# Re-ordering VectorE's top-k steps, loading second-MoE weight pieces ahead, and summing two slot tables on TensorE

## The chip, the cores and the metric

The kernel runs on one core of one Trainium2 chip, in one launch. The metric is device time in microseconds (us); smaller is better. The core has five engines with one in-order instruction queue each: TensorE (PE in the profile), VectorE (DVE), ScalarE (ACT), GpSimd (POOL) and SyncE (SP, which only issues DMAs here; POOL issues the indirect ones).

## The reference, cut to what matters

```python
scores = (q @ k.T) / sqrt(64)                # 4 batches, 8 heads, 576 rows
kth    = 32nd largest score of each row
attn   = softmax(where(scores >= kth, scores, -1e9)) @ v
x = attn as [2304 tokens, 512]
h = x @ w_in;  x = (h * clip(h + 3, 0, 6) / 6) @ w_out            # first MoE, d_ff 2048
logits = x @ w_gate;  e = argmax(logits);  g = softmax(logits)[e]   # 8 experts
out[t] = g[t] * (relu(x[t] @ w1[e]) @ w2[e])                     # second MoE, d_ff 1024
```

## The kernel before, in words

**Attention** goes in 144 tiles of 128 query rows (`T`), one per step of the loop at L1044. A step `t` works on several tiles at once, each at another stage: scores of tile t+2 on TensorE (`qk`) and their copy to SBUF on ScalarE (`sevac`); the search for the 32 largest of tile t on VectorE (`top_a`: eight MAX8 over 72 columns each at L626, then three MAX8 with two MATCH_REPLACE between them, L632 and L637); exponentials and a sign count of tile t-1 on ScalarE; then, for tile t-1, the scores not above the 24th largest (`z`). For the first 20 tiles (`ZPE`) z is made by GpSimd (L669) and TensorE (L596) in the PSUM tensor `yps`; for later ones by one VectorE instruction (L662). For tile t-2 `mask` then does three things on VectorE: MAX8 over z (L697, rank name `max8`), a small instruction that picks the 32nd value (L701, `match`), and the masking of the exponentials (L705, `mask`, two SBUF inputs of 576 columns). Transposes (L721) and the product with v (L755) follow on TensorE. In the first 200 us VectorE, ScalarE and GpSimd also convert the first MoE's weights from 64-bit to 32-bit numbers (`conv64`, L295 to L313).

**The order of the work** is made ahead of time by a planner. Every instruction has a rank: `pr0[0] + PRIO[name]`, where `pr0` grows by 400 a step. Among the instructions that its own model takes to be ready, the planner puts the lowest rank next into each engine's queue. At run time each queue is in order: an instruction whose input is late holds all those behind it.

**The first MoE** is cut into 144 steps (`moe_step`, 9 blocks of 256 tokens times 16 slices of d_ff) that run beside attention and alone after it, from about 850 us on: L829 (first matrix), ScalarE and VectorE (L835, L841), GpSimd (L264, L849), L860 (second matrix). Each step's piece of w_out is loaded by SP (L815). `gate` finds each token's expert, and GpSimd writes token numbers into one of two slot tables in DRAM (`td`, filled beforehand with values from 2304 up).

**The second MoE** takes the experts in turn, 384 token slots each. An expert's weights come in 8 pieces of 512 KB (`wpiece`): even numbers from w1, odd ones from w2. A piece is loaded by SP into one of three buffers `raw` (L967, L970), rounded by ScalarE (L977) and its remainder taken by VectorE (L978). Of expert 0, pieces 0, 2, 4, 6, 1 and 3 are asked for in the loop at L1112, while the first MoE ends; the converted pieces 5 and 7 lie in a pool (`tabp`) that opens only when the first MoE has ended. `load_table` (L951) reads the two tables and VectorE takes their minimum (L955). TensorE transposes it and adds the slots of the last block (L1133, L1135, into `tps`); VectorE turns the sum into the gather indices `tabg` (L1136) and the scatter indices `tab` (L1137). Three indirect DMAs of GpSimd gather the tokens of expert 0 (L1148); TensorE transposes them (L1157), ScalarE and VectorE round them (L1159, L1160), and the matrices follow (L1175, L1192).

Of the kernel before, what the change touches and what calls it, by code (L numbers as in the profile page):

```python
# [13 lines left out]
F32 = mybir.dt.float32  # L14
# [5 lines left out]
ALU = mybir.AluOpType  # L20
# [29 lines left out]
PRIO = dict(  # L50
    load=-1940, epi_a=370, top_c=55, exp=-295, need=75, qk=10, pv=-40, sevac=390, xevac=440, trans=210, xt0=75,
    tevac=450, xt1=-1170, l2=260, sign=175, epi_c=1010, wo=1175, prep=105, top8=270, rounds=-815, epi_b=165, l1=310,
    max8=315, match=560, mask=55, conv=295, xt2=-1335, z=365, gate=525, zw=60, zpe=70, yevac=405, convn=935,
)


# [1 line left out]
def attention_two_moe_kernel(  # L58
# [13 lines left out]
    PE, V, A, G, SP = nc.tensor, nc.vector, nc.scalar, nc.gpsimd, nc.sync  # L72

    B, H, S, D = q.shape
    NT, DM = out.shape
    F1 = w_in.shape[1]
    NE, _, F2 = w1.shape
    P = 128
# [13 lines left out]
    NG = NBLK * NF1  # L92
    YW = DM + 4
    NTT = NT // P
    SLOTS = 3
# [36 lines left out]
    def r_(ap):  # L132
        return ap.bitcast(F32)
# [7 lines left out]
    def run(gen):  # L141
        for _ in gen:
            pass

    cpool = ctx.enter_context(tc.tile_pool(name="cpool", bufs=1))
# [8 lines left out]
    def constants():  # L154
        c = {}
        c["ident"] = ident = cpool.tile([P, P], F32, name="ident")
        c["ntiny"] = ntiny = cpool.tile([P, 1], F32, name="ntiny")

        V.memset(ntiny, -1.02 * TINY2)
        c["one"] = one = cpool.tile([P, 1], F32, name="one")  # L160
        V.memset(one, 1.0)
        c["three"] = three = cpool.tile([P, 1], F32, name="three")
        V.memset(three, 3.0)
        c["tri"] = tri = cpool.tile([P, P], BF16, name="tri")

        make_identity(nc, ident)
        jp = cpool.tile([P, P], I32, name="jp")
        G.iota(jp, pattern=[[1, P]], base=0, channel_multiplier=-1)
        V.tensor_scalar(tri, jp, 0.0, None, op0=ALU.is_gt)
        c["ones"] = ones = cpool.tile([P, P], BF16, name="ones")  # L170
        V.memset(ones, 1.0)
        c["iota8"] = iota8 = cpool.tile([P, NE], F32, name="iota8")
        G.iota(iota8, pattern=[[1, NE]], base=0, channel_multiplier=0, allow_small_or_imprecise_dtypes=True)

        c["isum"] = isum = cpool.tile([P, 8, 2], F32, name="isum")
        G.iota(isum, pattern=[[2, 8], [-1, 2]], base=S - 2 * (TOPK - 1), channel_multiplier=0,
               allow_small_or_imprecise_dtypes=True)
        c["tok"] = tok = cpool.tile([P, NTT], F32, name="tok")
        G.iota(tok, pattern=[[P, NTT]], base=0, channel_multiplier=1, allow_small_or_imprecise_dtypes=True)


        c["row"] = row = cpool.tile([P, P], F32, name="row")
        G.iota(row, pattern=[[1, P]], base=0, channel_multiplier=0, allow_small_or_imprecise_dtypes=True)
        c["first"] = first = cpool.tile([P, NE, SLOTS], F32, name="first")
        G.iota(first, pattern=[[NT, NE], [P, SLOTS]], base=0, channel_multiplier=0, allow_small_or_imprecise_dtypes=True)
        c["tokm"] = tokm = cpool.tile([P, NTT], F32, name="tokm")
        G.iota(tokm, pattern=[[P, NTT]], base=-NT, channel_multiplier=1, allow_small_or_imprecise_dtypes=True)
        c["wg"] = wg = cpool.tile([P, NCC, NE], F32, name="wg")
        c["ohsum"] = cpool.tile([P, NE], BF16, name="ohsum")
        c["flag"] = cpool.tile([P, 2], F32, name="flag")  # L190
        c["ctl"] = cpool.tile([1, 2 + NE], I32, name="ctl")
        c["ctlf"] = cpool.tile([1, 2 + 2 * NE], F32, name="ctlf")
        return c
# [4 lines left out]
    def body(cs, exact):  # L198
        X = "x" if exact else ""
        ident, three, tri, ones, iota8 = cs["ident"], cs["three"], cs["tri"], cs["ones"], cs["iota8"]  # L200
# [747 lines left out]
        NSL = NE * SLOTS  # L948
        placed, gdone, trows, tables = [], [0], [], []

        def load_table():  # L951
            trows.extend(wp[0].tile([NSL, P], F32, name=f"trow{i}") for i in range(2))
            for a_, t_ in zip(trows, td):
                SP.dma_start(a_, t_.rearrange("(e s p) o -> e s (p o)", e=NE, p=P)[:, 0:SLOTS, :])
            V.tensor_tensor(trows[0], trows[0], trows[1], op=ALU.min)  # L955


        NPC = 4
        FW = F2 // NPC
        FPP = NF2 // NPC  # L960
        wst = {}

        def wpiece(e, i):
            kind, pc = i % 2, i // 2
            raw = wp[0].tile([P, 4 * FW], F32, tag="raw", bufs=3, name=f"raw{e}_{i}")
            if kind == 0:
                SP.dma_start(raw.rearrange("p (c f) -> p c f", c=NCC),  # L967
                             w1[e, :, pc * FW:(pc + 1) * FW].rearrange("(c p) f -> p c f", p=P))
            else:
                SP.dma_start(raw.rearrange("p (j n) -> p j n", j=FPP),  # L970
                             w2[e, pc * FW:(pc + 1) * FW, :].rearrange("(j p) n -> p j n", p=P))
            late = kind and pc >= NPC // 2
            nb = 3 if kind else 5
            pool = tabp[0] if late else wp[0]
            h = pool.tile([P, 4 * FW], F32R, tag=f"wh{kind}", bufs=nb, name=f"wh{e}_{i}")
            l = pool.tile([P, 4 * FW], F32R, tag=f"wl{kind}", bufs=nb, name=f"wl{e}_{i}")
            A.activation(h, raw, AF.Copy)  # L977
            V.tensor_tensor(l, raw, r_(h), op=ALU.subtract)  # L978
            wst[e, kind, pc] = (h, l)

        pend = []
        gpos = [0]
# [3 lines left out]
        def moe_step():  # L986
            g = gpos[0]
            if g >= NG + 3 or (g < NG and blkready[0] <= g // NF1):
                return
            gpos[0] += 1  # L990
            if 0 <= g - 1 < NG:
                epi_a(g - 1)
            yield
            if g >= 3:
                l2(g - 3)
                bk, f = divmod(g - 3, NF1)
                if f == NF1 - 1:
                    for tt, y in enumerate(yevac(bk)):
                        pend.append([gate(bk, tt, y), 0])
            yield  # L1000
            if 0 <= g - 1 < NF1:
                conv_upto(2 * (g - 1) + 1)
            if 0 <= g - 1 < NG:
                load_wo(g - 1)
            if 0 <= g - 2 < NG:
                epi_c(g - 2)
            yield
            if 0 <= g - 1 < NG:
                epi_b(g - 1)
            yield  # L1010
            if g < NG:
                if g < NF1:
                    conv_upto(2 * g)
                l1(g)
# [5 lines left out]
        wp, tabp = [None], [None]  # L1020

        def gate_step():
            for g_ in list(pend):

                if g_[1] or g_ is pend[0] or pend[0][1] > 2 or gpos[0] >= NG + 3:
                    g_[1] += 1
                    if next(g_[0], "end") == "end":
                        pend.remove(g_)
# [79 lines left out]
        at.close()  # L1108
        m2 = ExitStack()
        wp[0] = m2.enter_context(tc.tile_pool(name="wp" + X, bufs=1, side="right"))  # L1110
        pre = []
        while gpos[0] < NG + 3 or pend:  # L1112
            pr0[0] += STEP
            run(moe_step())
            gate_step()
            tc.cur_priority = pr0[0] + STEP
            if gdone[0] == NTT - TB // P and not trows:
                load_table()
            if gpos[0] > NG - 12 and len(pre) < NPC + NPC // 2:

                pre.append(2 * len(pre) if len(pre) < NPC else 2 * (len(pre) - NPC) + 1)
                wpiece(0, pre[-1])
        m1.close()
        tc.cur_priority = pr0[0] + 2 * STEP

# [3 lines left out]
        tab = tabp[0].tile([P, NSL], I32, name="tab")  # L1129
        tabg = tabp[0].tile([P, NSL], I32, name="tabg")  # L1130
        tps = ps2.tile([P, NSL], F32, tag="tp", bufs=2, name="tps")

        PE.matmul(tps, trows[0], ident[0:NSL, 0:NSL], start=True, stop=False)  # L1133
        for i, (a_, b_) in enumerate(placed):
            PE.matmul(tps, a_, b_, start=False, stop=(i == len(placed) - 1))  # L1135
        V.tensor_scalar(tabg, tps, float(NT - 1), None, op0=ALU.min)  # L1136
        V.tensor_copy(tab, tps)  # L1137

        xst = {}

# [63 lines left out]
        xgather(0)  # L1204
        for f_ in tables:
            f_()
        for i in range(2 * NPC):
            if i not in pre:
                wpiece(0, i)
# [3 lines left out]
        for s in range(len(seq) + 2):  # L1213
            if s < len(seq):
                e, f = seq[s]
# [33 lines left out]
    def more(cs, e, n):  # L1249
        ident = cs["ident"]  # L1250
        with ExitStack() as st:
# [10 lines left out]
            with tc.For_i(CAP, n, P) as i:  # L1262
# [31 lines left out]
                G.indirect_dma_start(out, bass.IndirectOffsetOnAxis(to, 0), o, None, bounds_check=NT - 1, oob_is_err=False)  # L1294

    cs = constants()
    body(cs, False)
    ctl = control(cs, "")
    big = P * (3 * T + 1) + NE
# [40 lines left out]
```

## Time and profile before

| | us |
|---|---|
| median of 3 runs | 1247.75 |
| lowest and highest of them | 1244.34, 1252.39 |
| the profiled execution: time | 1248.94 |
| the profiled execution: span | 1247.0 |
| TensorE matmul busy (92% of the span) | 1148.2 |
| VectorE busy (75%) | 940.1 |
| ScalarE busy (65%) | 816.1 |
| GpSimd busy (37%) | 461.8 |

The rows quoted below come from the profiled execution. Its span runs from the first to the last instruction; what the time holds beside it, 1.9 us, lies outside. Times in rows count from the start of the span. A row of a timeline gives start, length, engine, line, operation, output<-input, shape and count, and in brackets the idle time before it with what ended it.

### The profile page before, as it was taken

Reading aid. Unit: us, or ns where it says so; the run is one execution under the profiler, and the core shown is the slowest. Engines: PE = TensorE matmul, PEld = TensorE weight load, DVE = VectorE, ACT = ScalarE, POOL = GpSimd, SP = SyncE. Lnnn points to the kernel's source line nnn. Section 1 sums busy time; section 2 is a strip of 40 time slices with the busy share of each in tenths; the row PEclk is TensorE's granted clock in tenths of the full one; section 3 lists DMA queues with packets and bytes.
Section 4 is the critical chain, followed back from the end, with each engine's and each line's share of the span. In section 5 each row is a group of like instructions: output and inputs, shape, how many; then the busy total and the mean of one; then the engine's idle time right before and its main releaser. Section 6 shows DMA issues by size and latency. Waiting matters only on the chain.

```text
span 1247.0 us, 23972 instructions
## 1 busy us (share of the span) xinstructions
PE 1148.2 (92%) x7453; PEld 1033.9 (83%) x7453; DVE 940.1 (75%) x3800; ACT 816.1 (65%) x2089; POOL 461.8 (37%) x670
## 2 busy tenths in 40 slices
PE   6676788999999999999999999999986999999995
PEld 4565677788999899999888899998875999999994
DVE  4999999999999999999897999995423444444420
ACT  4888778687888887787777887784422444444421
POOL 5886555743323534323433323223433112221100
PEclk9678799999999999999999999999996999999998
DMA  3654556555544655645435545444954455555300
GB/s 81 201 163 137 181 187 207 156 140 144 148 125 126 141 155 161 141 124 135 129 99 153 145 121 155 121 121 125 315 170 136 147 171 172 154 163 164 121 19 26
DMA packets 184665, 180.22 MB, mean 145 GB/s; under 512 B 123933, under 2 KB 148813, under 8 KB 184528
## 3 DMA queue, kind: packets, MB, share of 16 engines
q1 hardware_dynamic: 178960, 167.24, 46.4%
q0 software_dynamic: 4416, 11.08, 2.9%
q8 instruction: 61, 1.00, 0.3%
q14 instruction: 76, 0.62, 0.2%
q10 hardware_dynamic: 1152, 0.28, 0.1%
HBM read 160.52 MB, written 19.59 MB: 144 GB/s over the span
## 4 chain that ended last, share of the span: by engine, by line
PE 74%; DVE 14%; ACT 5%; DMA 3%; issue 2%; POOL 2%; SPq 0%; POOLq 0%; ACTq 0%; DVEq 0%
PE l1ps L829 13%; PE yps L860 13%; PE lp L1175 11%; PE ops L1192 11%; PE ptps L755 9%; PE sps L596 5%; PE ptps L721 4%; DVE cd L626 2%; DVE pbuf L705 2%; DVE z L662 2%; DVE z L697 1%; PE ptps L888 1%; DMA raw<-in_moe_w_dram 1%; PE misc L440 1%; PE tp L1157 1%
## 5 line engine op out<-in xcount | busy, mean ns | idle before, releaser
L860 PE MATMUL yps<-wo,gh 128*128 128x512 f32 x576 | 216.3, 416 | 0.1
L264 POOL TENSOR_SCALAR gh<-gf 128x256 fp32r<-128x256 f32 x144 | 74.9, 520 | 348.9 <-PE yps L860 224.4
L626 DVE MAX8 cd<-sbuf 128x8 f32<-128x72 f32 x1152 | 187.9, 218 | 3.0 <-ACT sbuf L266 2.7
L829 PE MATMUL l1ps<-xh,wih 128*128 128x256 f32 x576 | 167.7, 291 | 8.7 <-DVE gf L841 6.6
L829 PE MATMUL l1ps<-xh,wil 128*128 128x256 f32 x576 | 163.8, 284 | 0.0
L829 PE MATMUL l1ps<-xl,wih 128*128 128x256 f32 x576 | 163.6, 284 | 0.0
L978 DVE TENSOR_TENSOR wl<-raw,wh 128x1024 fp32r<-128x1024 f32 x64 | 79.4, 1245 | 93.6 <-ACT wh L977 91.7
L755 PE MATMUL ptps<-vn,pt 128*128 128x65 f32 (+1 forms) x1152 | 145.1, 280 | 0.0
L755 PEld LDWEIGHTS ptps<-vn,pt 128*128 128x128 f32 x1152 | 142.4, 200 | 0.0
L705 DVE SCALAR_TENSOR_TENSOR pbuf<-sbuf,tall,pbuf 128x576 f32<-128x576 f32 x144 | 137.2, 953 | 0.2
L849 POOL TENSOR_TENSOR gl<-gf,gh 128x256 fp32r<-128x256 f32 x144 | 124.8, 867 | 11.3
L829 PEld LDWEIGHTS l1ps<-xh,wih 128*128 128x128 f32 x576 | 110.0, 191 | 20.1 <-DVE gf L841 12.3
L977 ACT ACTIVATE wh<-raw 128x1024 fp32r<-128x1024 f32 x64 | 67.7, 1059 | 83.4 <-PE lp L1175 40.2
L860 PEld LDWEIGHTS yps<-wo,gh 128*128 128x128 f32 x576 | 107.2, 189 | 16.0 <-POOL qh L452 0.3
L860 PE MATMUL yps<-wo,gl 128*128 128x512 f32 x288 | 116.6, 405 | 0.6 <-POOL gl L849 0.6
L687 ACT ACTIVATE jk<-sbuf,uall 128x576 bf16<-128x576 f32 x144 | 111.6, 775 | 4.1 <-DVE j L701 0.9
L678 ACT ACTIVATE pbuf<-sbuf,nb 128x576 f32<-128x576 f32 x144 | 111.1, 775 | 4.1 <-PE ptps L723 0.9
L829 PEld LDWEIGHTS l1ps<-xl,wih 128*128 128x128 f32 x576 | 110.1, 191 | 4.1
L266 ACT ACTIVATE sbuf<-sps 128x576 f32<-128x576 f32 x144 | 93.0, 646 | 29.9 <-PE sps L596 17.9
L721 PE MATMUL ptps<-ident,pbuf 128*128 128x128 f32 x576 | 93.7, 285 | 18.1 <-DVE j L701 10.2
L829 PEld LDWEIGHTS l1ps<-xh,wil 128*128 128x128 f32 x576 | 110.3, 192 | 0.1
L596 PE MATMUL sps<-kx,qh 128*128 128x288 f32 (+2 forms) x336 | 95.8, 318 | 15.0 <-ACT sbuf L266 11.1
(206 smaller groups left out, 3043.0 us busy)
## 6 DMA issues: line engine op xcount, KB each, us to landing
wo<-wod SPq DMA_DIRECT2D x144, 512.0 KB
raw<-in_moe_w_dram SPq DMA_DIRECT2D x64, 512.0 KB
vn<-in_v_dram SPq DMA_DIRECT2D x96, 128.0 KB
rawi<-in_moe_w_in_dram SPq DMA_DIRECT2D x16, 512.0 KB
rawo<-in_moe_w_out_dram SPq DMA_DIRECT2D x16, 512.0 KB
wod<-wc SPq DMA_DIRECT2D x16, 512.0 KB
qn<-in_q_dram SPq DMA_DIRECT2D x126, 64.0 KB
yd<-y SPq DMA_DIRECT2D x18, 258.0 KB
```

The costliest lines, as they stand in the source:

```text
L596: PE.matmul(d_, a_, b_, start=(i == 0), stop=(i == len(mm) - 1))
L626: V.max(cd[:, c, :], s[:, c * CK:(c + 1) * CK])
L678: A.activation(d["p"], d["s"], AF.Exp, bias=d["nb"], scale=SCALE)
L687: A.activation(jk, d["s"][:, 0:S], AF.Sign, bias=ts[t]["u"], scale=-1.0, accum_out=d["sg"])
L705: V.scalar_tensor_tensor(d["p"], d["s"], tall[:, t:t + 1], d["p"], op0=ALU.is_ge, op1=ALU.mult)
L721: PE.transpose(ptps[:, c * P:(c + 1) * P], pb[:, c0 + c * P:c0 + (c + 1) * P], ident)
L755: PE.matmul(d_, a_, b_, start=(i == 0), stop=(i == len(mm) - 1))
L829: PE.matmul(dst, a[:, c, fs], b_[:, c, :], start=(n == 0), stop=(n == 3 * NCC - 1))
L849: G.tensor_tensor(gl, gf, r_(gh), op=ALU.subtract)
L860: PE.matmul(yps[tt], a[:, tsl], b_, start=(f == 0 and m == 0), stop=(f == NF1 - 1 and m == 2))
L1175: PE.matmul(lp, a[:, c, fs], b_[:, c, :], start=(n == 0), stop=(n == 3 * NCC - 1))
L1192: PE.matmul(ops_[j], a[:, js], b_[:, ns], start=(f == 0 and m == 0), stop=(f == NF2 - 1 and m == 2))
```

## The change

In attention five ranks change: the MAX8 over z and the pick of the 32nd value go ahead of where they were, z too; the masking of the exponentials goes from rank 55 to rank 305, behind the next tile's eight MAX8 (rank 270); the weight conversion goes from 295 to 330.

For the second MoE the load of a piece is split from its conversion (`wload_`, `wpiece`). In the loop at L1112 the loads run three pieces ahead of the conversions and start one step earlier. Pieces 5 and 7 of expert 0 are no longer loaded as soon as a buffer is free: GpSimd first copies one column of the first gathered token tile into their buffer, so their loads wait until that gather has landed.

The two slot tables are no longer combined by VectorE. TensorE adds both into `tps`, and VectorE subtracts a constant, `empty`, which is what an untouched entry holds; the indices are made from the difference `tabf`.

```diff
-    max8=315, match=560, mask=55, conv=295, xt2=-1335, z=365, gate=525, zw=60, zpe=70, yevac=405, convn=935,
+    max8=-40, match=300, mask=305, conv=330, xt2=-1335, z=290, gate=525, zw=60, zpe=70, yevac=405, convn=935,
...
+        c["empty"] = empty = cpool.tile([P, NE, SLOTS], F32, name="empty")
+        G.iota(empty, pattern=[[NT, NE], [P, SLOTS]], base=NT, channel_multiplier=1, allow_small_or_imprecise_dtypes=True)
...
-            V.tensor_tensor(trows[0], trows[0], trows[1], op=ALU.min)
...
-        def wpiece(e, i):
+        wraw = {}
+
+        def wload_(e, i, after=None):
             kind, pc = i % 2, i // 2
-            raw = wp[0].tile([P, 4 * FW], F32, tag="raw", bufs=3, name=f"raw{e}_{i}")
+            wraw[e, i] = raw = wp[0].tile([P, 4 * FW], F32, tag="raw", bufs=3, name=f"raw{e}_{i}")
+            if after is not None:
+                G.tensor_copy(raw[:, 0:1], after[:, 0:1])
             if kind == 0:
                 SP.dma_start(raw.rearrange("p (c f) -> p c f", c=NCC),
...
+        def wpiece(e, i):
+            kind, pc = i % 2, i // 2
+            if (e, i) not in wraw:
+                wload_(e, i)
+            raw = wraw.pop((e, i))
...
-        pre = []
+        pre, order = [], [0, 2, 4, 6, 1, 3, 5, 7]
...
-            if gpos[0] > NG - 12 and len(pre) < NPC + NPC // 2:
-
-                pre.append(2 * len(pre) if len(pre) < NPC else 2 * (len(pre) - NPC) + 1)
-                wpiece(0, pre[-1])
+            if gpos[0] > NG - 13 and len(pre) < NPC + NPC // 2:
+
+                if len(wraw) == 3 or len(pre) + len(wraw) == NPC + NPC // 2:
+                    pre.append(order[len(pre)])
+                    wpiece(0, pre[-1])
+                if len(pre) + len(wraw) < NPC + NPC // 2:
+                    wload_(0, order[len(pre) + len(wraw)])
...
-        PE.matmul(tps, trows[0], ident[0:NSL, 0:NSL], start=True, stop=False)
+        for i, a_ in enumerate(trows):
+            PE.matmul(tps, a_, ident[0:NSL, 0:NSL], start=(i == 0), stop=False)
         for i, (a_, b_) in enumerate(placed):
             PE.matmul(tps, a_, b_, start=False, stop=(i == len(placed) - 1))
-        V.tensor_scalar(tabg, tps, float(NT - 1), None, op0=ALU.min)
-        V.tensor_copy(tab, tps)
+        tabf = tabp[0].tile([P, NSL], F32, name="tabf")
+        V.tensor_tensor(tabf, tps, cs["empty"].rearrange("p e s -> p (e s)"), op=ALU.subtract)
+        V.tensor_scalar(tabg, tabf, float(NT - 1), None, op0=ALU.min)
+        V.tensor_copy(tab, tabf)
...
         xgather(0)
         for f_ in tables:
             f_()
+        for i in range(2 * NPC):
+            if i not in pre and (0, i) not in wraw:
+                wload_(0, i, xst[0][3][0])
         for i in range(2 * NPC):
             if i not in pre:
                 wpiece(0, i)
```

## Rows read from the trace of the kernel before

**Rows 1.** Busy us by stretch: PE, PEld, DVE, ACT, POOL; clock, DMA share, GB/s.

```profile
25.00:250.00 225.00, 175.02 (x1058) 150.03 (x1059) 214.84 (x830) 174.97 (x460) 151.62 (x153) 0.86 0.57 174
...
300.00:850.00 550.00, 545.34 (x4008) 503.64 (x4007) 514.46 (x2409) 438.92 (x1228) 188.54 (x310) 1.00 0.50 136
850.00:950.00 100.00, 84.58 (x547) 73.70 (x545) 38.22 (x130) 35.19 (x82) 40.13 (x64) 0.93 0.60 187
950.00:1232.00 282.00, 280.09 (x1440) 252.81 (x1440) 115.24 (x142) 112.85 (x165) 48.17 (x66) 0.99 0.43 135
```

**Rows 2.** Waits of TensorE, 25 to 250 us: total us, times, longest.

```profile
PE ptps L721 <- DVE j L701: 8.9, 9, 2.9
...
PE yps L596 <- DVE z L697: 8.1, 6, 2.2
```

**Rows 3.** Waits of TensorE, 900 to 957 us.

```profile
PE tp L1157 <- POOL gw L1161: 7.8, 1, 7.8
PE l1ps L829 <- DVE gf L841: 3.1, 2, 1.7
```

**Rows 4.** The chain of waits, 900 to 925 us: start, us, what.

```profile
903.26 7.00 DMA raw<-in_moe_w_dram
...
912.63 5.19 DMA raw<-in_moe_w_dram
```

**Rows 5.** SP's queue by time, three of the weight-piece loads after 895 us.

```profile
896.71 0.39 SPq L970 DMA_DIRECT2D raw<-in_moe_w_dram  x1
...
946.12 0.38 SPq L970 DMA_DIRECT2D raw<-in_moe_w_dram  x1
947.25 0.81 SPq L967 DMA_DIRECT2D raw<-in_moe_w_dram  x1
```

**Rows 6.** ScalarE's timeline, the last two conversions of expert 0.

```profile
943.77 2.00 ACT L977 ACTIVATE wh<-raw 128x1024 fp32r<-128x1024 f32 x2 [3.85 <-DMA td<-tok,ad]
```

**Rows 7.** GpSimd's timeline, the first gather of expert 0.

```profile
944.49 0.99 POOL L1148 DMA_INDIRECT xg<-yd,tabg  x1 [0.85 <-issue]
```

**Rows 8.** The page's DMA issues, one row.

```profile
raw<-in_moe_w_dram SPq DMA_DIRECT2D x64, 512.0 KB
```

**Rows 9.** Busy us by stretch, while the gathers land.

```profile
950.00:952.00 2.00, 1.09 (x4) 0.72 (x4) 0.00 (x0) 0.01 (x1) 0.19 (x1) 0.50 1.04 408
```

**Rows 10.** TensorE's timeline, the slot table.

```profile
940.75 0.59 PE L1133 MATMUL tps<-ident,trow 24*128 24x24 f32 x2 [0.45 <-DVE ad L923]
942.01 1.05 PE L1135 MATMUL tps<-oh,oh 128*128 128x24 f32 x4 [0.67 <-DVE oh L933]
```

**Rows 11.** GpSimd's timeline at the start: an iota, and the idle time after.

```profile
2.03 0.24 POOL L185 IOTA first<- 128x24 f32 x1
...
11.68 0.29 POOL L408 TENSOR_SCALAR ke<-ke 64x128 fp32r<-64x128 f32 x1 [8.32 <-PE yps L415]
```

**Rows 12.** The chain of waits: second matrix of expert 0, slice 4.

```profile
980.15 2.06 PE ops L1192 x9
```

**Rows 13.** VectorE's timeline, the gather indices.

```profile
943.49 0.18 DVE L1136 TENSOR_SCALAR tabg<-tps 128x24 int32<-128x24 f32 x1 [1.14 <-DMA yd<-y]
```

**Rows 14.** The masking by line (ns min/median/max), then its busy time to 150 us.

```profile
L705 DVE SCALAR_TENSOR_TENSOR pbuf<-sbuf,tall,pbuf x144: 794/811/1944, 23.5 to 859.7; 128x576 f32<-128x576 f32 x144
...
0.00:150.00 150.00, 21.10 (x19) 0.82 0.51 146
```

**Rows 15.** Timelines: a masking beside GpSimd's subtraction, another beside its z.

```profile
76.96 1.29 POOL L313 TENSOR_TENSOR wil<-cvi,wih 128x512 fp32r<-128x512 f32 x1
...
77.38 1.48 DVE L705 SCALAR_TENSOR_TENSOR pbuf<-sbuf,tall,pbuf 128x576 f32<-128x576 f32 x1
...
59.94 2.21 POOL L669 TENSOR_SCALAR z<-sbuf,uall 128x576 bf16<-128x576 f32 x1 [0.21 <-ACT uall L650]
...
60.61 0.80 DVE L705 SCALAR_TENSOR_TENSOR pbuf<-sbuf,tall,pbuf 128x576 f32<-128x576 f32 x1
```

**Rows 16.** Waits of VectorE, 25 to 250 us.

```profile
DVE z L697 <- PE yps L596: 1.9, 1, 1.9
```

## The prediction

> **What bounds the kernel now.** I read busy time by stretch first, then the waits of the engine that is short in each stretch, then the chain of waits where TensorE has holes. From 300 to 850 us TensorE is busy 545.3 of 550 us and VectorE 514.5; from 950 to 1232 us TensorE 280.1 of 282 [rows 1]. There no order of other work can give back more than TensorE's holes, 4.7 and 1.9 us. From 25 to 250 us it is the other way round: VectorE is busy 214.8 of 225 us, TensorE 175.0, at a granted clock of 0.86 [rows 1]. TensorE's waits for VectorE there (8.9 us for the 32nd value, 8.1 us for the search in z [rows 2]) are mostly the lot of an engine that isn't the bound. Between 850 and 950 us TensorE loses 15.4 us [rows 1]. Two holes of this, 3.1 us together, are first-MoE steps that wait for VectorE's gf, and 7.8 us are one wait for the first gathered tokens [rows 3]. The chain of waits leads the two small holes back to two weight loads, of 7.00 and 5.19 us [rows 4]: ScalarE's in-order queue stood at a piece's conversion until the load had landed, with the first MoE's activation behind it.
>
> **The change part by part.**
>
> *Loads ahead.* Those two loads are not pieces 0 to 3 of expert 0; counted in the queue they are the first two of expert 1. They are late because the two loads before them, pieces 5 and 7 of expert 0 (the second is issued at 896.71 [rows 5]), keep two of the three buffers until they are converted at 943.77 [rows 6]. The change takes pieces 5 and 7 out of this stretch, so three buffers circulate, 1.05 MB less is moved in it, and the first six pieces have three steps between load and conversion. Gain: the 3.1 us of the two holes. Bounds: nothing, if the conversions are planned earlier by as much as the loads (the stall then only moves), and 3.1 us, since there is no more to win. I take 3.1, as both causes go.
>
> *Two pieces behind the gather.* At 946.12 and 947.25 two loads start on the buffers that the conversions at 943.77 freed [rows 5, 6], in the middle of the gathers, the first of which is issued at 944.49 [rows 7]. They are 512 KB each [rows 8], and while they land all queues together move 408 GB/s [rows 9]: 1.05 MB / 408 GB/s = 2.6 us of DMA time, an estimate of what the gathers were held up. In the changed kernel pieces 5 and 7 are loaded after the first gather, so most of this goes. Bounds: nothing, if the gathers are limited by their own descriptors, and 5.4 us, which is the 7.8 us wait less the 1.4 us from the table's last matmul (943.06 [rows 10]) to the issue and less the issue itself, 0.99 [rows 7]. I take 2.6. The wait added stands in GpSimd's queue as two one-column copies, about the 0.24 us of a 24-column GpSimd instruction each [rows 11]; behind them stand copies that wait for the same gather, and gathers of expert 1, wanted after 990 us. SP has behind its two loads only pieces of expert 1. Pieces 5 and 7 themselves are first used in slice 4 of the second matrix, at 980.15 [rows 12], some 30 us after the gather; a load of 7.00 us and the conversions fit, so they cost nothing. If this cover went, a late piece would cost its lateness in full.
>
> *Tables.* The added matmul is one of the size of the two rows of 0.59 us [rows 10], some 0.3 us, and runs while TensorE waits 0.67 us for the last block's slots [rows 10]: nothing. VectorE's minimum of the two reads leaves a queue that has idle time there: nothing (VectorE is busy 38.2 of 100 us there [rows 1]). On the path to the gather one VectorE instruction of the size of tabg's is added, 0.18 us [rows 13]: 0.2 us lost. The added constant is an iota of 24 columns, 0.24 us, ahead of 8.32 us in which GpSimd is idle [rows 11]: nothing.
>
> *Ranks.* No instruction is added or removed; VectorE does the same work in another order. Where VectorE is the bound, 25 to 250 us, order can give back its idle time, 225 - 214.8 = 10.2 us [rows 1], and the time it loses to GpSimd; it can also lose more of both. After that TensorE is the bound, and VectorE's 35.5 us of slack to 850 us [rows 1] covers a worse order. I take 0 for it: the masking goes later by about one group of MAX8, the search in z sooner, and its users (TensorE's transposes) are two steps behind. The bounds are -10.2 us and what the collisions below can add.
>
> *The rule on the shared port.* The masking has two SBUF inputs. Alone it takes 0.81 us (median), at most 1.94 [rows 14]; beside GpSimd's subtraction of the weight conversion it took 1.48 us [rows 15]. Beside GpSimd's z at 59.94 it took 0.80 [rows 15], no longer than alone. In the first 150 us 19 maskings took 21.1 us [rows 14], 1.11 each, so 5.7 us went there in collisions. The Trainium skill (SBUF — State Buffer, "SBUF: two separate sides") says that a VectorE instruction with two SBUF inputs and a GpSimd instruction that reads SBUF exclude each other for a whole instruction, the first to start keeping the other out. By that rule moving the masking trades its collisions for others, and a later masking that met GpSimd each time would give rival B's 1258; the subtraction's row agrees with it, the row beside z does not, and by that one the sum stays at 1242. The sum by bounds from the rows: all 19 collisions gone, -5.7 us (within the 10.2 and the busy time beside it); all 19 at the longest, 19 x (1.94 - 1.11) = +15.8 us.
>
> **Sum.** Against the profiled time of 1248.94 us: -3.1 - 2.6 + 0.2 + 0 = -5.5, which gives 1243.4. That execution lies 1.2 us above the median of the runs, 1247.75, so 1242 on the scale of the median.
>
> **Rivals.**
>
> *A, faster than that: the new order pays where VectorE is the bound.* For it: 8.1 us in which TensorE stood before the single z buffer until VectorE had searched it [rows 2], which the earlier search shortens, and 10.2 us of VectorE idle time. Against it: VectorE waited only 1.9 us for TensorE's z there [rows 16], so most of TensorE's waits are not VectorE's. With all of the 10.2 us: 1242 - 10 = 1232. With half of it 1237.
>
> *B, slower than before: the masking meets GpSimd more often.* The place is the first 250 us, where the conversion's subtractions and z run on GpSimd and VectorE has no slack. If each of the 19 maskings takes 1.94 us, 15.8 us are added: 1258, 10 us slower than before. It decides from 5.5 us on, that is 0.29 us more per masking; below that the gains at the end outweigh it. To be slower by 1%, 18 us in all, the same would have to reach the other VectorE instructions of the conversion too. For it: a maximum of 1.94 us that exists. Against it: the masking beside z at 59.94 wasn't longer, and a later masking may as well miss a subtraction as meet one.
>
> *C, nothing comes of the loads.* The DMA engines are busy 0.60 of the time from 850 to 950 us [rows 1], more than in the stretches around it; the planner places conversions by its own idea of a load's length, and the holes may come back at another piece; and a conversion of piece 5 or 7 put ahead of the rounding of the gathered tokens in ScalarE's queue would hold the first matrix until its load, up to 7.00 us [rows 4], has landed, which eats the gather's gain. Then 1247.75 + 0.2, say 1248.
>
> **How the numbers follow.** The forecast (gains at the end, neutral order) gets 0.5, with a range of its own of 1237 to 1247; A 0.22; B 0.11; C 0.17. The predicted time is 1242. The range reaches down to A with nearly all of its idle time, 1231, and up to B without its extreme, 1256. About 1% is what a measurement of this kernel can tell from no change: faster by that is under 1235.3, slower over 1260.2. Most of A and a thin edge of the forecast are faster by 1%: 0.22. The far end of B, with collisions beyond the masking, is slower by 1%: 0.09. The rest, 0.69, is within.
>
> **What would show it.** Loads: no wait of TensorE for gf between 900 and 925 us, and the first two loads of expert 1 issued before 903 us. Gather: TensorE's wait for the first tokens down from 7.8 us to about 5.2, with no weight load between the first gather's issue and its landing. Tables: one more instruction of about 0.2 us between the last matmul of the table and tabg. Ranks: VectorE's busy time from 25 to 250 us unchanged within a few us, the masking's mean in the first 150 us near 1.11 us (towards 0.81 for A, 1.9 for B), and the first MoE alone from about 850 us on as now. Wrong would be a step of attention that is longer or shorter throughout 300 to 850 us: then the order changed something in the stretch where I take TensorE to be the bound.

## The result, and the profile after

The changed kernel took 1261.61 us (median of 6 runs, 1259.13 to 1263.92) against 1249.78 us for the kernel before (median of 6 runs): ratio 1.0097, 95% interval 1.007 to 1.0124. The forecast was 1242 us, range 1231 to 1256. The change makes the kernel slower, beyond the upper end of that range. The profiled execution has a span of 1258.8 us against 1247.0, 11.8 us more.

**Where the time went.** Busy us by stretch of the changed kernel (PE, PEld, DVE, ACT, POOL; granted clock, DMA share, GB/s), the same four stretches as [rows 1]:

```profile
25.00:250.00 225.00, 164.93 (x976) 140.40 (x977) 196.28 (x779) 165.63 (x435) 136.69 (x135) 0.81 0.53 163
300.00:850.00 550.00, 545.76 (x4022) 505.28 (x4021) 516.82 (x2420) 443.90 (x1245) 187.38 (x318) 1.00 0.50 136
850.00:950.00 100.00, 95.14 (x629) 83.71 (x629) 43.39 (x164) 40.45 (x102) 35.90 (x64) 0.98 0.57 169
950.00:1232.00 282.00, 273.06 (x1391) 247.41 (x1392) 121.11 (x163) 114.62 (x165) 54.95 (x74) 0.97 0.46 147
```

From 300 to 850 us the busy times stay: TensorE is busy 545.8 of 550 us, before 545.3. The first row changed: VectorE, which bounds that stretch, was busy 214.84 of 225 us before and is now busy 196.28. It didn't get more work; it stands idle. The last two rows are the same work some 10 us later.

The start of the n-th masking (L705 before, L707 after), read from VectorE's timelines, is a mile post for each tile (us; the masking itself now goes one group of MAX8, 1.2 us, later within its step):

| masking | 6th | 11th | 16th | 21st | 41st | 81st | 144th |
|---|---|---|---|---|---|---|---|
| before | 64.56 | 96.92 | 124.51 | 160.02 | 288.39 | 508.20 | 859.72 |
| after | 73.40 | 109.47 | 139.35 | 174.86 | 303.95 | 525.02 | 872.42 |
| later by | 8.8 | 12.6 | 14.8 | 14.8 | 15.6 | 16.8 | 12.7 |

So nearly all of the loss, 14.8 us, is made by the 16th tile. Two more us are added by the 81st, and 4 come back by the 144th. The tiles in which it is made are among the first 20, whose z GpSimd makes (`ZPE`).

**What the engines wait for there.** Waits of TensorE from 25 to 150 us (total us, times, longest), in the changed kernel:

```profile
PE yps L598 <- POOL z L671: 20.0, 14, 2.2
PE yps L598 <- DVE m L634: 8.6, 2, 4.7
```

and in the kernel before:

```profile
PE yps L596 <- DVE z L697: 8.1, 6, 2.2
...
PE yps L596 <- POOL z L669: 1.7, 2, 1.1
```

The direction of the dependence has turned round. Before, TensorE came to z's product in `yps` when GpSimd's z had long been there, and stood six times for VectorE's search that had to free `yps`. Now it stands for GpSimd. The second row of the changed kernel is the same wait: its two matmuls, at 63.51 and 84.60 us, start 0.05 us after a z of GpSimd ends, and a VectorE instruction that ended at about the same time got the name. So it is 16 waits, 28.6 us in total. The first of those two:

```profile
61.20 2.26 POOL L671 TENSOR_SCALAR z<-sbuf,uall 128x576 bf16<-128x576 f32 x1
...
63.51 0.40 PE L598 MATMUL yps<-z,identb 128*128 128x288 bf16 x1 [3.97 <-DVE m L634]
```

VectorE's waits in the same stretch of the changed kernel:

```profile
DVE z L699 <- PE yps L598: 9.5, 8, 2.7
DVE j L703 <- ACT pt L268: 7.7, 7, 1.8
```

The first was 1.9 us, once [rows 16]; the second is in no row of before from 25 to 150 us. Together they are 15.3 us more, about the 14.3 us by which VectorE's busy time from 25 to 150 us fell (116.38 to 102.06).

One step shows how. A timeline of the changed kernel, all engines (start, length, engine, line, instruction, idle time before):

```profile
64.69 0.45 PE L598 MATMUL yps<-kx,ql 128*128 128x288 f32 x1
65.17 0.77 DVE L699 MAX8 z<-yps 128x8 f32<-128x576 f32 x1 [1.71 <-PE yps L598]
...
66.72 2.21 POOL L671 TENSOR_SCALAR z<-sbuf,uall 128x576 bf16<-128x576 f32 x1 [1.22 <-ACT uall L652]
...
68.99 0.40 PE L598 MATMUL yps<-z,identb 128*128 128x288 bf16 x1 [1.40 <-POOL z L671]
...
71.04 1.06 PE L723 MATMUL ptps<-ident,pbuf 128*128 128x128 f32 x4
...
72.35 0.70 ACT L268 ACTIVATE pt<-ptps 128x640 f32<-128x640 f32 x1 [1.08 <-PE ptps L725]
...
73.09 0.23 DVE L703 SCALAR_TENSOR_TENSOR j<-ptps,sg,z 128x16 f32<-128x16 f32 x1 [1.33 <-ACT pt L268]
```

GpSimd's z ends at 68.93, and `yps` starts at 68.99: it was already at the head of TensorE's queue. Behind it stand the transposes of another tile, behind these ScalarE's copy `pt`, and behind that VectorE's pick `j`, before which VectorE is idle for 1.33 us (the pick reads a constant that the program keeps in the PSUM tensor of the transposes, `ptps`). At 65.17 the search itself waited, 1.71 us, and started 0.03 us after the last matmul into `yps`. In the kernel before, the z that GpSimd made from 59.94 to 62.15 [rows 15] goes into `yps` at 64.11, 2 us after it was there, and VectorE's search of the z before goes without a wait, 3.83 us after its last matmul:

```profile
58.73 0.44 PE L596 MATMUL yps<-kx,ql 128*128 128x288 f32 x1
...
63.00 0.74 DVE L697 MAX8 z<-yps 128x8 f32<-128x576 f32 x1
...
64.11 0.46 PE L596 MATMUL yps<-z,identb 128*128 128x288 bf16 x1
```

The timelines show the same in tile after tile. From the 6th to the 20th, the matmul into `yps` started 2.6 us (median) after GpSimd's z was done in the kernel before, and starts 0.05 us after it in the changed one. VectorE's search started 3.7 us (median; 0.4 to 4.8) after the last matmul into `yps` before, and starts 0.3 us (0.03 to 1.6) after it now. So the old order left some 6 us of room in most tiles, and the new one leaves almost none.

**The masking** isn't it. Its row of the changed kernel by line, and its busy time to 150 us, beside [rows 14]:

```profile
L707 DVE SCALAR_TENSOR_TENSOR pbuf<-sbuf,tall,pbuf x144: 792/809/1829, 23.4 to 872.4; 128x576 f32<-128x576 f32 x144
```
```profile
0.00:150.00 150.00, 17.34 (x17) 0.77 0.45 132
```

1.02 us each, before 1.11: less was lost in it, not more.

**The end.** The end of the last `yps` matmul of the first MoE moves from 932.06 to 941.51, by 9.5 us, and the last masking moved by 12.7: between the two 3.2 us are won. The waits of TensorE for gf, 3.1 us in [rows 3], are down to one of 0.2 us. SP's queue of the changed kernel, the last of the six early loads and the next:

```profile
899.65 0.39 SPq L975 DMA_DIRECT2D raw<-in_moe_w_dram  x1
...
950.31 0.88 SPq L972 DMA_DIRECT2D raw<-in_moe_w_dram  x1
```

Between them no weight piece is loaded at all; before, loads were issued at 903.26 and 912.63, among others [rows 4]. The win isn't the loads' alone, since the ranks change this stretch too: with equal ranks it is 2.3 us (72.34 before, 70.04 in *e2* below) or 4.8 (73.92 in *e1*, 69.09 in the changed kernel). From the end of the last `yps` matmul to the second MoE's second matrix it is 31.66 us (941.51 to 973.17), before 30.34: 1.3 us lost. TensorE's wait for the first gathered tokens is what it was, 7.8 us [rows 3]:

```profile
PE tp L1174 <- POOL raw L970: 7.8, 1, 7.8
```

### The profile page after: what moved, and what is told of

Its sections match the earlier page's. It is cut to its first block, busy times and chain, and to the rows that moved or that the text cites. A ratio compares the mean times of both kernels' runs of the same rounds, so it can differ in the third digit from the quotient of the medians.

```text
span 1258.8 us, 23975 instructions
## 1 busy us (share of the span) xinstructions
PE 1151.3 (91%) x7455; PEld 1038.2 (82%) x7455; DVE 937.6 (74%) x3800; ACT 816.6 (65%) x2089; POOL 452.1 (36%) x673
## 4 chain that ended last, share of the span: by engine, by line
PE 69%; DVE 15%; POOL 5%; ACT 5%; issue 3%; DMA 2%; SPq 0%; POOLq 0%; ACTq 0%; DVEq 0%
PE l1ps L831 12%; PE yps L862 11%; PE lp L1192 11%; PE ops L1209 10%; PE ptps L757 8%; PE sps L598 5%; PE ptps L723 4%; POOL z L671 3%; DVE cd L628 2%; DVE pbuf L707 2%; DVE z L699 2%; PE yps L598 2%; DVE z L664 1%; DVE cw L639 1%; DVE m L634 1%
## 5 line engine op out<-in xcount | busy, mean ns | idle before, releaser
L266 POOL TENSOR_SCALAR gh<-gf 128x256 fp32r<-128x256 f32 x144 | 66.9, 464 | 351.6 <-PE yps L862 204.6
L757 PE MATMUL ptps<-vn,pt 128*128 128x65 f32 (+1 forms) x1152 | 140.2, 274 | 0.0
L757 PEld LDWEIGHTS ptps<-vn,pt 128*128 128x128 f32 x1152 | 136.9, 194 | 0.0
L707 DVE SCALAR_TENSOR_TENSOR pbuf<-sbuf,tall,pbuf 128x576 f32<-128x576 f32 x144 | 133.6, 928 | 0.1
L268 ACT ACTIVATE pt<-ptps 128x640 f32<-128x640 f32 (+1 forms) x144 | 94.7, 658 | 17.9 <-PE ptps L725 16.1
L664 DVE SCALAR_TENSOR_TENSOR z<-sbuf,uall 128x576 f32<-128x576 f32 x124 | 106.0, 855 | 0.0
```

The costliest lines, as they stand in the source:

```text
L268: A.activation(dst, src, AF.Copy)
L664: V.scalar_tensor_tensor(d["z"], s, d["u"], s, op0=ALU.is_le, op1=ALU.mult)
L707: V.scalar_tensor_tensor(d["p"], d["s"], tall[:, t:t + 1], d["p"], op0=ALU.is_ge, op1=ALU.mult)
L757: PE.matmul(d_, a_, b_, start=(i == 0), stop=(i == len(mm) - 1))
```

## The experiments

Theory P: the search in z, with its new rank, goes into the queues as soon as the planner has z ready, and in the first 20 tiles the real z of GpSimd, 2.21 us, isn't there yet. (What the planner's model takes for that z is in no trace; this half of P is inferred from where the instructions stand.) Rival Q: the order of masking and pick by itself, or collisions of the masking with GpSimd. Rival R: the loads, the gather and the tables. No kernel leaves out any of the computation. Line numbers differ a little between the kernels; the names tell the instruction. Ratios are to the kernel before, on the same chip, with a 95% interval.

**Which part of the change.** *e1* is the kernel before with the ranks alone, *e2* the changed kernel with the old ranks, *e3* the kernel before with one of the five ranks.

```diff
-    max8=315, match=560, mask=55, conv=295, ... z=365,      (e2: these back in the changed kernel)
+    max8=-40, match=300, mask=305, conv=330, ... z=290,     (e1: these in the kernel before; e3: max8=-40 alone)
```

> The kernel before with the five new ranks and nothing else. Theory P (the ranks cost the time, in the first 20 tiles: the search in z is put into VectorE's queue and TensorE's z matmuls into TensorE's as soon as the plan has z ready, and both stand until GpSimd's z of 2.2 us is done): 12 to 15 us slower than the kernel before, with TensorE's waits for GpSimd's z near 20 us from 25 to 150 us (1.7 before). Rival R (the loads, the gather or the tables cost it): within 3 us of the kernel before.

> The changed kernel with the five old ranks: the loads ahead, the two pieces behind the gather and the tables alone. Theory P: attention ends when it did before, and the result is 0 to 4 us faster than the kernel before (3.1 us of the two holes gained, some of it given back around the gather). Rival R: 8 us or more slower.

> The kernel before with one rank changed, the search in z from 315 to -40. Theory P: most of the loss, 8 to 15 us slower, with TensorE's waits for GpSimd's z of 15 us or more from 25 to 150 us. Rival Q (the later masking and the earlier pick of the 32nd value, which waits for ScalarE): within 3 us of the kernel before.

e1: 1266.85 against 1250.65 us, 1.0131 (1.0085 to 1.0177). e2: 1248.70, 0.9976 (0.9958 to 0.9994). e3: 1269.65, 1.0153 (1.0116 to 1.0191). The ranks cost 16 us, the rest of the change gains 2, and their sum, +14, agrees with the measured +12 within the intervals. The rank of the search alone costs as much, 19.0 us, more than the 8 to 15 that were expected. TensorE's waits for GpSimd's z from 25 to 150 us, in e1, e2 and e3:

```profile
PE yps L596 <- POOL z L669: 19.1, 13, 2.1
```
```profile
PE yps L598 <- POOL z L671: 1.8, 2, 1.1
```
```profile
PE yps L596 <- POOL z L669: 20.5, 14, 2.4
```

As in the changed kernel, waits for the same z that another name got come on top: 8.2 us in e1, 3.4 in e3, none in e2. With e1 and e2 R falls. With e3 Q falls as the only cause, since masking and pick have their old ranks there.

**Is it GpSimd's z?** In *e5* and *e6* VectorE makes z in all tiles, with the old ranks and with the new.

```diff
-ZPE = 20
+ZPE = 0          (e5: kernel before;  e6: kernel before with the five new ranks)
```

> The kernel before with ZPE = 0: z of the first 20 tiles is made by one VectorE instruction like that of the others, so neither GpSimd nor TensorE takes part in it. It is the base for the next run. All theories: VectorE is the bound in that stretch, and 20 instructions of 0.8 us are added to it, so some 10 to 20 us slower than the kernel before.

> The same with the five new ranks. Theory P (the new ranks cost time only where the search waits for a z that comes from GpSimd and TensorE): within 4 us of the run with ZPE = 0 and the old ranks. Rival Q (the later masking and the earlier pick cost it): 10 us or more slower than that run.

e5: 1262.59 against 1251.53 us, 1.0092 (1.0068 to 1.0116). e6: 1252.90, 1.0013 (0.9999 to 1.0027). Without GpSimd's z the same five ranks make the kernel 9.7 us faster; with it, 16 us slower. P had expected no difference beyond 4 us, so its number missed; but Q, which had expected a loss of 10, falls, and the core of P stands: the order isn't bad by itself, and the loss needs the z that comes from other engines. The gain is what rival A of the prediction hoped for, in a kernel that A wasn't about.

**Only where z is VectorE's own.** *e4* is the changed kernel with the old rank of the search in the first 20 tiles, *e9* the changed kernel with all five old ranks until the step in which tile 20 is searched, *e8* is e2 with max8=-40 from tile 20 on.

```diff
-    pr("max8")
+    pr("max8" if t >= ZPE else "max8e")                   (e4; max8e=315)
...
+    rank = OLD[name] if name in OLD and tnow[0] < ZPE + 2 else PRIO[name]    (e9, in pr; OLD: the five old ranks)
```

> The changed kernel, but the search in z keeps its old rank, 315, for the first 20 tiles (those whose z GpSimd and TensorE make) and has -40 only after them. Theory P: the loss is gone, 0 to 5 us faster than the kernel before. Rival Q: still 8 us or more slower.

> The changed kernel with the old ranks, except that the search in z has -40 from tile 20 on. Theory P: where VectorE makes z itself the early search costs nothing, so within 2 us of the changed kernel with the old ranks (2 us faster than the kernel before). Rival Q says the same, since masking and pick have their old ranks. If the early search itself is bad everywhere: 5 us or more slower.

> The changed kernel, with all five ranks as before up to the step in which tile 20 is searched in z, and the new ones from there on. Theory P: all that the ranks cost lies in the first 20 tiles, so the time is within 2 us of the changed kernel with the old ranks, 1 to 4 us faster than the kernel before. If the other four ranks also cost something in the later tiles: 3 us or more slower than the kernel before, as with the early search taken back alone.

e4: 1254.32 against 1250.65 us, 1.0024 (1.0006 to 1.0042). e8: 1250.44 against 1251.53, 0.9996 (0.9979 to 1.0013). e9: 1245.05 against 1252.66, 0.9941 (0.9921 to 0.9962). In e4 the other ranks are still new in the first tiles, and part of the wait stays; in e9 it is gone. TensorE from 25 to 150 us in e4 and in e9:

```profile
PE yps L598 <- POOL z L671: 11.3, 7, 3.2
```
```profile
PE yps L602 <- POOL z L675: 0.4, 1, 0.4
```

So the search's rank is enough for the loss (e3), but not the only rank that makes it. e4 came out between the two forecasts, 3.7 us slower than the kernel before. It and e9 differ only in the first 20 tiles, by the ranks of pick, masking and conversion (z's rank, 365 or 290, acts on none of them: there z is made under `zw` and `zpe`, which the change left alone), and by their ratios that is some 10 us. Which of the three ranks does it was not tried. e8 came out as expected, and e9 beats both kernels, by more than the 1 to 4 us that were expected. Its lead over e2, 3.5 thousandths, has intervals that just touch (0.9958 to 0.9962); e8, which keeps only one new rank late, shows no lead. The traces do show an effect of the late order: from the 81st masking to the 144th it is 347.4 to 347.9 us in each of the seven traces with all five new ranks there (the changed one, e1, e4, e6, e9, e10, e12), and 349.7 to 351.5 in the other seven traces. But TensorE does less in that stretch (2522 matmuls in e9, 2538 in e2), so part of the work is only moved. How much of the 3 to 4 us is left at the end stays open.

**Through whose queue?** In *e10*, the kernel before with the five new ranks, `yps` on TensorE gets a late rank, so that less stands behind its wait.

```diff
-    ... zpe=70, ...
+    ... zpe=350, ...
```

> The kernel before with the five new ranks, and the rank of TensorE's z matmuls raised from 70 to 350, so that they stand behind the scores (10), the transposes (210) and the like in TensorE's queue. If the loss comes through TensorE's queue (its z matmuls stand at GpSimd's z, 19 to 20 us, and hold the scores and transposes behind them): at least half of it is gone, less than 8 us slower than the kernel before. If it comes through VectorE's queue alone (its search stands at z): still 12 us or more slower.

e10: 1262.91 against 1252.66 us, 1.0075 (1.0057 to 1.0093). Some 10 us are left of 16, and the intervals of e10 and e1 overlap. TensorE's wait for GpSimd's z fell by a third, from 27.3 us in e1 to 18.3, of which 14.7 stand in this row and 3.6 under another name:

```profile
PE yps L596 <- POOL z L669: 14.7, 10, 2.1
```

and VectorE's own wait for `yps` stayed (10.7 us, in e1 10.1). Neither number that was expected came. The edit took only part of TensorE's wait away, so it doesn't separate the two queues: how the loss is split between TensorE's and VectorE's is not settled.

**The end of the change.** *e7* is e2 with pieces 5 and 7 not held behind the gather, *e11* is e2 with the first piece of expert 1 held as well, *e12* joins e11's hold to e9.

```diff
-                wload_(0, i, xst[0][3][0])
+                wload_(0, i)                              (e7)
...
+        wload_(1, 0, xst[0][3][0])                        (e11, e12: after the two loads)
```

> The changed kernel with the old ranks, but pieces 5 and 7 of expert 0 load as soon as a buffer is free, not behind the first gather. If what was gained at the end (the two holes of 3.1 us) came from taking these two pieces and those behind them out of the first MoE's tail, the holes are back and the time is that of the kernel before within 2 us. If it came from loading three pieces ahead, the holes stay away and it is 2 to 4 us faster than the kernel before.

> The changed kernel with the old ranks, and the first piece of expert 1 put behind the first gather too, so that no weight load lies beside the last store of the first MoE's result. If that load delays the store and with it the gather: the first gather is issued 0.5 to 1.2 us sooner after the last matmul of the first MoE, and the kernel is 2 to 4 us faster than the kernel before. If not: the same as with the old ranks alone, 2 us faster.

> The two edits that beat the kernel before, together: the five new ranks only from the step in which tile 20 is searched (alone 1245.05 against 1252.66, 0.9941), and the first piece of expert 1 held behind the first gather as well (alone over the ends 0.9961 where the ends without it gave 0.9976). Theory P: the first has its whole effect in the attention, the second behind the last yps matmul, so they add: about 1.5 us less than with the first alone, ratio 0.992 to 0.994, gather issued about 11.5 us behind the last yps matmul (12.7 with the first alone), the search waiting under 2 us for GpSimd's z in 25 to 150 us. Rival: the hold only moves the load into the gathers and TensorE's first transposes wait for it as long (first gather to first transpose 7 us and not 6): ratio as with the first alone, 0.9941 or worse.

e7: 1252.95 against 1251.53 us, 1.0008 (0.9989 to 1.0027). The two holes are back although the loads run three pieces ahead (TensorE, 895 to 960 us):

```profile
PE l1ps L831 <- DVE gf L843: 3.3, 2, 2.1
```

So it is the hold of pieces 5 and 7 that removes them, not the lead of the loads. The hold also does what was hoped of it behind the gather: from the first gather's issue to TensorE's first transpose it is 7.89 us in e7 and 5.69 in e2. But the issue itself, counted from the end of the last `yps` matmul, is 0.9 us later in e2 (12.08 and 13.02).

e11: 1248.13 against 1252.66 us, 0.9961 (0.9946 to 0.9976); e12: 1244.79 against 1249.59, 0.995 (0.9934 to 0.9966). Why the gather is issued later is seen in the timelines of e2, all engines:

```profile
935.79 1.87 PE L890 MATMUL ptps<-wg,yt 128*128 128x8 f32 x8 [0.27 <-ACT lg L898]
...
938.76 0.91 SPq L919 DMA_DIRECT2D yd<-y  x2
...
939.71 0.46 SPq L972 DMA_DIRECT2D raw<-in_moe_w_dram  x1
...
940.89 1.05 PE L1150 MATMUL tps<-oh,oh 128*128 128x24 f32 x4 [0.29 <-DVE oh L935]
...
943.00 0.18 DVE L1152 TENSOR_TENSOR tabf<-tps,empty 128x24 f32<-128x24 f32 x1 [1.77 <-DMA yd<-y]
...
944.30 0.99 POOL L1165 DMA_INDIRECT xg<-yd,tabg  x1 [1.78 <-DMA raw<-in_moe_w_dram]
```

and of e11:

```profile
934.67 1.24 PE L890 MATMUL ptps<-wg,yt 128*128 128x8 f32 x8 [0.27 <-ACT lg L898]
...
937.00 0.90 SPq L919 DMA_DIRECT2D yd<-y  x2
...
939.13 1.05 PE L1150 MATMUL tps<-oh,oh 128*128 128x24 f32 x4 [0.29 <-DVE oh L935]
...
940.39 0.18 DVE L1152 TENSOR_TENSOR tabf<-tps,empty 128x24 f32<-128x24 f32 x1 [0.92 <-PE tps L1150]
...
941.68 0.99 POOL L1165 DMA_INDIRECT xg<-yd,tabg  x1 [0.93 <-DVE tab L1154]
```

In e2 (and in the changed kernel) the next weight piece starts right behind the stores of the tokens, and the table waits for the stores, 1.06 us beyond TensorE's last matmul for it. With that piece held it is 0.21 us in e11; e12 still waits for the stores, 0.47 us against 0.84 in e9. Where the table waits for the stores, it starts 4.0 to 4.2 us after they are issued with the piece beside them (changed kernel, e2, e4, e8, e9) and 3.6 without it (kernel before, e12), so the piece seems to cost some 0.4 to 0.6 us. From the end of the last `yps` matmul to the first gather's issue it is 12.43 us before, 13.17 after, 13.02 in e2, 12.71 in e9, 11.48 in e11 and 11.57 in e12. Not all of what the hold seems to win is the hold's: 0.63 us of the 1.54 between e2 and e11, and 0.78 of the 1.14 between e9 and e12, lie before the stores, in the last eight matmuls of `gate` (1.87 and 1.24 us in the rows above), where TensorE's granted clock falls to 0.50 a little earlier in one run than in the other (0.57 from 935 to 937 us in e2, 0.85 from 934 to 936 in e11). And the time isn't measurably shorter for it: the intervals of e11 and e2 overlap. From that matmul to the second matrix: 30.34 before, 31.66 after, 31.93 in e2, 30.55 in e9, 30.78 in e11, 30.42 in e12. What e12 wins over e9 at the issue, 1.1 us, it gives back behind it, 0.9 us of it in the first 36 matmuls of `lp` (7.45 us in e9, 8.33 in e12), which run at a granted clock of 0.50 for longer. From 950 to 955 us in e9 and in e12:

```profile
950.00:955.00 5.00, 5.00 (x25) 4.77 (x25) 4.28 (x6) 3.67 (x5) 2.94 (x4) 0.83 0.79 238
```
```profile
950.00:955.00 5.00, 5.00 (x20) 4.54 (x19) 3.65 (x4) 2.98 (x4) 2.38 (x5) 0.56 1.02 359
```

The forecast of the rival that was written for e12, no sum, came, but not its mechanism: from the first gather to the first transpose it is 6.24 us in e12 and 6.13 in e9, not 7 (in e11 it is 6.95, against 5.69 in e2). e9 and e12 are the best versions, and can't be told apart.

## Why the prediction was wrong

The step that failed is the term of the ranks, "I take 0 for it: the masking goes later by about one group of MAX8, the search in z sooner, and its users (TensorE's transposes) are two steps behind." It cost 16.2 us (e1). The step followed the moved instruction to its users, and not to its input. In 20 of 144 tiles that input is made by GpSimd in 2.21 us and carried by TensorE, and the stretch of these tiles is the one where VectorE has no slack, as the first part of the prediction says. The upper bound for the ranks, 15.8 us, is near by luck: it was worked out from longer maskings, and these became shorter (1.02 us each, 1.11 before).

The row that should have warned was read the wrong way. VectorE's single wait of 1.9 us for `yps` [rows 16] was used against rival A, as a sign that VectorE was seldom held. But a row of waits doesn't say how much room there is where nobody waits. That one wait ended at 29.39 us, in the third tile; from the 6th tile to the 20th the search came 3.7 us (median) after its z was in `yps`. The rank moved it by 355 of the 400 that a step counts, and a step took 6.4 us there ((160.02 - 64.56) / 15): an estimate of 5.6 us, more than the 3.7. None of the rivals had this mechanism: A had the order paying, B had the masking lengthened, C had the loads.

*Loads ahead*: about the 3.1 us that were predicted. The holes of 3.1 us are gone, 3.3 us of them are back in e7, and the stretch from the last masking to the last `yps` matmul is 2.3 us shorter with the old ranks (e2). Of the two causes given, pieces 5 and 7 in this stretch is right; the three steps between load and conversion do nothing alone (e7). The sign to look for was wrong: expert 1's first loads did not come before 903 us but at 950.31, behind the stores.

*Two pieces behind the gather*: 2.6 us were expected and nothing came. Against e7 the hold itself wins 2.2 us behind the issue of the gather and loses 0.9 before it; against the kernel before the two cancel. From the first gather's issue to TensorE's first transpose it is 0.7 us less (6.37 before, 5.64 after), and the issue is 0.7 us later, since a load of expert 1 now starts right behind the stores, where none stood before. This is the second term that was mis-sized: -2.6 became 0. Up to the second matrix it is even +1.3, because the first 36 matmuls of `lp` run slower (6.62 us before, 8.41 after); the transposes and the rounding before them give 0.6 of that back (5.08 us, 4.43). With the old ranks the change is worth -2.0 us (e2) where -5.5 were summed.

*Tables*: right. One instruction of 0.18 us more on the path; nothing else shows.

*The rule on the shared port* did not decide this: the masking's mean fell to 1.02 us. But the prediction read one masking beside z, and there are two kinds. In the two traces up to 150 us, 13 maskings that began 0.67 us or more after GpSimd's z had begun and ran beside it took 0.80 or 0.81 us; five of the changed kernel, which began 0.07 to 0.37 us after it, took 1.20 to 1.29. The Trainium skill (SBUF — State Buffer, "SBUF: two separate sides") states that a VectorE instruction with two SBUF inputs and a GpSimd instruction that reads SBUF keep each other out for the whole instruction. These times agree with it for the start of z only: z takes 2.21 us or more, and none of the 18 waited for its end. No run here moved the masking alone.

*What would show it* did its work: VectorE's busy time from 25 to 250 us was to stay "unchanged within a few us", and it fell by 18.6 us, which named the place at once. The steps of attention after 300 us stayed nearly as they were: 568.5 us from the 41st masking to the 144th, before 571.3.

## What to carry to other kernels

Where an order is planned from modelled durations and queues are in order, an instruction that is moved forward is priced by its input, not by its users: look up who makes it, how long that takes in the trace, and how long the input has lain there, tile by tile, when the instruction starts. That is the room, and it is to be set against how far the new rank moves the instruction. A row of waits doesn't show it: here 1.9 us of waiting stood beside 3.7 us of room, and the move took more than that. Ask this for each stretch in which the input has another maker; a rank that does no harm in most tiles can be wrong for the first 20, and a switch at that tile (e9) turned +0.97% into -0.59%. When loads are taken away from beside a critical transfer, look which load the queue issues next in their place.

## What was not expected of the hardware

The granted clock at the start of the second MoE comes back at different times in kernels that do the same work there: the first 36 `lp` matmuls take 6.62 us before, 7.45 in e9, 7.80 in e11, 8.33 in e12 and 8.50 in e2, and the earlier issue of the first gather in e12 (1.1 us, counted from the last `yps` matmul) did not bring the full clock sooner than in e9. It falls at different times too, at the end of the first MoE: the last eight matmuls of `gate` take 1.06 us in e12, 1.24 in e11, 1.84 in e9 and 1.87 in e2. In all of these it stands at 0.50 (1.2 GHz) while TensorE waits some 8 us for the first tokens, and rises to 1.00 (2.4 GHz) while it runs the `lp` matmuls one behind the other. What decides the moment, of the fall or of the rise, was not found. So a difference of a microsecond there, between two traces, can be the clock's and not the edit's.
